# The y sums of the first batch with both halves of the channels side by side, in an order made anew

## The chip, the core and the metric

One core of a Trainium2 chip runs the kernel. TensorE (PE) multiplies matrices, and its weight loads are listed as PEld; VectorE (DVE), ScalarE (ACT) and GpSimd (POOL) do the rest of the arithmetic, and SyncE (SP) issues the transfers. The metric is the time on the device in microseconds (us), as a median of runs.

## The reference, cut to what matters

The program is an attention, a mixing of tokens, and a gated block, for 2 batches of 768 tokens and 512 channels. All arithmetic is float32. The change lies in the middle part:

```
x = attention(q, k, v)                # windows of 16 keys and 24 block summaries; 8 heads of 64
theta = x @ w_theta
zr, zi = x * cos(theta), x * sin(theta)
y = einsum('ts,bsd->btd', w_tok_r, zr) + einsum('ts,bsd->btd', w_tok_i, zi)
u = x + y
x = u + max(u @ w_ch, 0)              # then the gated block: w_in, gelu, layer norm, w_sg, w_out
```

## The kernel before

Every float32 product is made of three matmuls: each operand is split into a high and a low part (`mm3`, lines 650 to 652). `x` is kept transposed in `xT`, channels on the partitions.

**The attention** has 16 units: 8 pairs of heads (`at_pair`), each in 2 halves of the tokens (`at_unit`). A unit is a chain through the engines: scores `S` on PE, row maxima `m` and differences `P` on DVE, the exponential on ACT, transposes `PT` on PE, their copies `Pt`, the values `O` on PE, the normalisation (`ri`, then `x`) on DVE, a transpose `X` on PE and its copy into `xT`. The scores of all units share one pair of PSUM banks (kind "S" of the pools; the six other banks are of kind "B"), so that a unit's scores wait for the differences of the unit before. `k`, `q`, `vT` and `v` of each unit come by DMA, as do all weights.

**The mixing.** For each block of 128 tokens `n` (6 for each batch) `theta` makes `th` on PE; ACT and DVE take off whole turns (`kk`, `rr`). For each half of the channels, `h`, `rotated` makes sine and cosine (tile `f`), multiplies them by `x`, and splits the products into high and low (tile `z`). `mixed` adds a block's `z` into the sums. The output of a 128-channel group `d` has 768 tokens: the first 512 lie in a bank `y`, the other 256 (the rest) in half of a bank `ys`. A step of the sums is six matmuls, three of 512 columns into `y` and three of 256 into `ys`, and there are two steps (weights `w_r` and `w_i`) for each of the two groups of a half:

```
for i in range(NT):                 # NT = 6 blocks of tokens
    for j in range(2):              # d = 2 * h + j
        for k_, key_ in enumerate(("r", "i")):
```

Before, `mixed` runs once for each batch and half: all six blocks for the first half of the channels, then all six for the second. It holds three banks at a time. When the last step is done, DVE adds the sums to `xT` (`uv`).

**The order** of all instructions is made when the program is built. `Order.play` is a planner: each operation has estimated costs, a due time (`key`, drawn from the table `PLAN` or from what depends on it, less a lead from `LEAD`), and a shift of its own (`SHIFT`). The planner plays the engines forward and takes, on each, the most urgent operation that could start soon. Where PE would idle between 6 and 36 us of its reckoning, it puts in dummy matmuls (`fill_B`, from `filler`). `gates` hold back the making of `z` so that it isn't more than a few blocks ahead of the sums.

After the mixing come `ch` (the product with `w_ch`), `iv` and `iu` (the two halves of `w_in`), `Qs` (the product with `w_sg`), and `o` (`w_out`), whose parts are stored as they are done.

Of the kernel before, what the change touches and what calls it, by code (L numbers as in the profile page):

```python
# [22 lines left out]
NT = S // P  # L23
# [25 lines left out]
    Qz=74.168, ks=-40.136, vs=-11.881, vm=11.936, vr=-13.929, e=17.901, Pt=48.07, n=-10.669,  # L49
    xe=4.677, xh=9.148, xl=4.343, kk=-1.1, rr=-29.76, sc=-13.602, zm=-9.187, zh=7.556, zl=38.914,  # L50
    w_tht=8.728, w_rt=13.865, w_it=-1.048, w_rit=-8.999, k=-3.022, q=-3.059, v=1.199, vT=9.157,
    w_rd=22.528, w_id=-5.655, w_rid=3.014, w_thd=-9.579, bsg=-5.815, ch_e=13.7, d=14.634,
    gagf=-1.524, gh=8.649, gl=15.226, gm=-10.408, iu_g=88.574, iv_g=-16.768, m=-33.701,
    o_e=-19.883, rv=-3.588, sq=1.118, st=-55.633, tx=-19.318, tx_h=10.785, u=-3.396, u_h=-9.153,
    uv=-43.926, vh=6.864, vl=9.675, vo=-7.023, vp=0.039, w_chd=6.133, w_chh=-0.456, w_chl=3.459,
    w_chr=-13.975, w_cht=58.117, w_ih=-5.761, w_il=-46.919, w_inud=10.646, w_inuh=12.592,
    w_inul=-13.707, w_inur=8.343, w_inut=57.665, w_invd=15.806, w_invh=-50.158, w_invl=-21.398,
    w_invt=-8.855, w_ir=22.177, w_outd=-25.619, w_outh=15.605, w_outl=-21.45, w_outr=6.525,
    w_outt=12.079, w_rh=5.347, w_rih=6.258, w_ril=-15.3, w_rir=-13.172, w_rr=-12.082,
    w_sgd=9.125, w_sgh=5.251, w_sgl=6.738, w_sgsd=-2.394, w_sgsh=-4.109, w_sgsl=-4.009,  # L60
    w_thh=-3.486, ab=-11.929, o_ae=-17.964, o_be=5.444, w_invr=-3.314, w_rl=6.746, w_thl=8.414,
    w_thr=-2.869, Qaa=-36.615, Qab=18.479, Qac=-4.476, Qad=32.953, Qba=-7.182, Qbb=-4.881,
    Qbc=-45.244, Qbd=0.242, Qd=-14.617, Qe=15.488, Qg=4.768, Qh=-3.207, Qk=-11.256, Ql=5.491,
    Qm=10.937, Qu=-4.014, Qv=11.136, Qw=28.942, Qxh=5.023, Qxl=-5.36, gc=0.703, gt=2.997,
    gw=24.853, Qn=-29.771, Qx=-8.957, Qyh=1.69, Qyl=-22.283)
# [4 lines left out]
    warm0=(3.965, 0), masks0=(-3.862, 0), sets=(3.556, 0), masks2=(1.455, 0),  # L70
    cst=(15.845, 2.915), fill=(-9.642, 0), w_th0d=(-3.673, 15.198), w_th0t=(2.45, 0),
    w_th0r=(-.408, 0), w_th0h=(-1.22, 0), w_th0l=(.268, 0), w_th1d=(-1.914, -18.157),
    w_th1t=(1.029, 0), w_th1r=(-1.741, 0), w_th1h=(1.156, 0), w_th1l=(-.234, 0),
    w_th2d=(1.529, 5.971), w_th2t=(1.909, 0), w_th2r=(-1.914, 0), w_th2h=(-1.157, 0),
    w_th2l=(-.108, 0), w_th3d=(4.03, -1.082), w_th3t=(-2.527, 0), w_th3r=(-.575, 0),
    w_th3h=(-1.077, 0), w_th3l=(1.202, 0), w_r0d=(-.168, -2.081), w_r0t=(.588, 0),
    w_r0r=(-1.087, 0), w_r0h=(1.116, 0), w_r0l=(-1.655, 0), w_i0d=(-1.155, 15.003),
    w_i0t=(4.861, 0), w_i0r=(1.493, 0), w_i0h=(.108, 0), w_i0l=(-1.832, 0),
    w_ri0d=(3.082, -21.492), w_ri0t=(-7.525, 0), w_ri0r=(-.588, 0), w_ri0h=(-4.096, 0),
    w_ri0l=(-4.15, 0), w_r1d=(2.146, 10.79), w_r1t=(2.919, 0), w_r1r=(-1.704, 0),  # L80
    w_r1h=(-1.983, 0), w_r1l=(-1.058, 0), w_i1d=(-1.983, 11.44), w_i1t=(.641, 0),
    w_i1r=(4.405, 0), w_i1h=(-1.438, 0), w_i1l=(3.002, 0), w_ri1d=(.07, -2.92),
    w_ri1t=(-5.223, 0), w_ri1r=(.001, 0), w_ri1h=(-.079, 0), w_ri1l=(5.236, 0),
    w_r2d=(-7.111, -10.609), w_r2t=(.053, 0), w_r2r=(4.47, 0), w_r2h=(-5.26, 0),
    w_r2l=(-2.052, 0), w_i2d=(11.782, -14.445), w_i2t=(4.916, 0), w_i2r=(-.222, 0),
    w_i2h=(1.104, 0), w_i2l=(-1.867, 0), w_ri2d=(-1.883, 3.84), w_ri2t=(-.804, 0),
    w_ri2r=(-.544, 0), w_ri2h=(-5.231, 0), w_ri2l=(-2.723, 0), w_r3d=(-1.364, -8.117),
    w_r3t=(-3.117, 0), w_r3r=(4.499, 0), w_r3h=(-7.344, 0), w_r3l=(-5.466, 0),
    w_i3d=(7.147, 1.379), w_i3t=(-2.77, 0), w_i3r=(-5.827, 0), w_i3h=(-8.506, 0),
    w_i3l=(4.281, 0), w_ri3d=(-12.998, -22.098), w_ri3t=(1.16, 0), w_ri3r=(-2.26, 0),  # L90
    w_ri3h=(.737, 0), w_ri3l=(.496, 0), w_r4d=(6.596, -7.956), w_r4t=(-4.96, 0), w_r4r=(.092, 0),
    w_r4h=(.009, 0), w_r4l=(-10.529, 0), w_i4d=(-11.202, -6.738), w_i4t=(-1.817, 0),
    w_i4r=(-8.488, 0), w_i4h=(-1.595, 0), w_i4l=(.021, 0), w_ri4d=(6.591, -2.316),
    w_ri4t=(-.414, 0), w_ri4r=(1.569, 0), w_ri4h=(-3.272, 0), w_ri4l=(4.015, 0),
    w_r5d=(12.123, 3.875), w_r5t=(-2.799, 0), w_r5r=(.332, 0), w_r5h=(-.403, 0),
    w_r5l=(-12.426, 0), w_i5d=(8.685, 2.603), w_i5t=(2.874, 0), w_i5r=(-10.224, 0),
    w_i5h=(7.798, 0), w_i5l=(-2.331, 0), w_ri5d=(1.821, -1.805), w_ri5t=(-2.508, 0),
    w_ri5r=(6.718, 0), w_ri5h=(-.537, 0), w_ri5l=(3.889, 0), w_ch0d=(19.331, -7.138),
    w_ch0t=(6.055, 0), w_ch0r=(.748, 0), w_ch0h=(-3.195, 0), w_ch0l=(2.036, 0),
    w_inv0d=(9.499, -8.007), w_inv0t=(5.274, 0), w_inv0r=(.996, 0), w_inv0h=(4.98, 0),  # L100
    w_inv0l=(-2.049, 0), w_inu0d=(-13.818, -1.564), w_inu0t=(-1.458, 0), w_inu0r=(-2.338, 0),
    w_inu0h=(-.759, 0), w_inu0l=(-2.165, 0), w_out0d=(15.204, -.19), w_out0t=(-1.162, 0),
    w_out0r=(2.291, 0), w_out0h=(.433, 0), w_out0l=(-1.945, 0), w_ch1d=(16.728, -2.047),
    w_ch1t=(7.412, 0), w_ch1r=(2.329, 0), w_ch1h=(-5.061, 0), w_ch1l=(-2.158, 0),
    w_inv1d=(4.343, 25.037), w_inv1t=(4.333, 0), w_inv1r=(-4.484, 0), w_inv1h=(-6.68, 0),
# [441 lines left out]
def kernel(  # L547
# [106 lines left out]
    def sl(c, n=P):  # L654
        return slice(c * n, (c + 1) * n)
# [944 lines left out]
```

## Time and profile before

| what | us |
|---|---|
| median of 3 runs | 382.21 |
| lowest and highest of them | 379.33, 382.38 |
| the profiled execution, whole | 380.85 |
| its span, first to last instruction | 379.1 |
| PE busy in the span | 369.4 |
| DVE, ACT, POOL busy | 261.6, 204.1, 120.1 |

The profile is of one execution; 1.75 us of its time lie outside its span. A matmul's end is modelled, so that rows of consecutive matmuls overlap by some tenths of a microsecond, and the pitch is read from start to start. "Issue" in a column of waits means that no event in the profile explains the wait.

### The profile page before, as it was taken

The page shows a single profiled execution, that of the slowest core. Times are in us where ns is not written, and L with a number is a line of the kernel's source. Part 1 is how long each engine was busy: PE and PEld are TensorE (multiplying, and loading weights), DVE is VectorE, ACT ScalarE, POOL GpSimd, SP SyncE. Part 2 cuts the span into 40 slices and gives each one's busy share as a digit, 9 for nine tenths or more (in the row PEclk, how much of TensorE's full clock was granted, in tenths as well). Part 3 has the DMA queues.
Part 4 walks back from the last instruction along what each step waited for, and adds up shares of the span by engine and source line. Part 5 has one row for each costly group of instructions (what it writes and reads, how often), then busy time and mean ns, then how long its engine had stood idle before and what let it go on. Part 6 is the DMA issues. An engine that isn't in the chain of part 4 may idle for free.

```text
span 379.1 us, 7679 instructions
## 1 busy us (share of the span) xinstructions
PE 369.4 (97%) x2991; PEld 321.9 (85%) x2991; DVE 261.6 (69%) x453; ACT 204.1 (54%) x349; POOL 120.1 (32%) x145
## 2 busy tenths in 40 slices
PE   8898999999999999999999999999999999999996
PEld 4786888888888888888888788888888999999996
DVE  4997999999975964436674968684134487689621
ACT  2586699967874862234743862458234876332100
POOL 6663488553310200002620163335000046521000
PEclk9998999999999999999999999999999999999999
DMA  7999897992005041002556921646021443511222
GB/s 267 334 338 305 297 315 191 316 345 70 0 9 215 2 145 62 2 0 80 182 171 240 355 99 64 228 158 218 0 83 43 125 144 106 158 52 58 91 103 84
DMA packets 27332, 57.38 MB, mean 151 GB/s; under 512 B 3424, under 2 KB 16800, under 8 KB 27296
## 3 DMA queue, kind: packets, MB, share of 16 engines
q1 hardware_dynamic: 27296, 56.90, 44.9%
q8 instruction: 23, 0.38, 0.4%
q14 instruction: 13, 0.11, 0.1%
HBM read 45.18 MB, written 11.40 MB: 149 GB/s over the span
## 4 chain that ended last, share of the span: by engine, by line
PE 82%; DMA 5%; DVE 5%; ACT 3%; issue 2%; POOL 1%; SPq 1%; POOLq 0%; DVEq 0%; ACTq 0%
PE y L650 6%; PE y L651 6%; PE y L652 6%; PE Qs L650 3%; PE Qs L651 3%; PE Qs L652 3%; PE ch L650 3%; PE ys L651 3%; PE ch L651 3%; PE ys L652 3%; PE iu L652 3%; PE iu L651 3%; PE ch L652 3%; PE iu L650 3%; PE iv L652 3%; PE iv L651 3%
## 5 line engine op out<-in xcount | busy, mean ns | idle before, releaser
L645 DVE TENSOR_TENSOR z<-f,z 128x512 fp32r<-128x512 f32 x21 | 14.9, 709 | 20.8 <-ACT z L637 20.6
L650 PE MATMUL Qs<-Qx,Qh 128*128 128x384 f32 x84 | 28.2, 336 | 0.2 <-DVE U L1458 0.2
L652 PE MATMUL Qs<-Qx,Ql 128*128 128x384 f32 x84 | 28.1, 334 | 0.0
L651 PE MATMUL Qs<-Qx,Qh 128*128 128x384 f32 x84 | 28.1, 334 | 0.0
L652 PE MATMUL ys<-w_ri,z 128*128 128x256 f32 x96 | 27.1, 282 | 0.0
L651 PE MATMUL ys<-w_ri,z 128*128 128x256 f32 x96 | 27.1, 282 | 0.0
L650 PE MATMUL ys<-w_ri,z 128*128 128x256 f32 x96 | 26.7, 278 | 0.0
L637 ACT ACTIVATE z<-f 128x512 fp32r<-128x512 f32 x19 | 11.9, 627 | 23.7 <-PE ys L652 18.1
L650 PEld LDWEIGHTS ys<-w_ri,z 128*128 128x128 f32 x96 | 18.0, 188 | 4.4
L637 ACT ACTIVATE Qx<-Qx 128x768 fp32r<-128x768 f32 x20 | 16.6, 843 | 9.3 <-DMA Qx<-dQx 6.4
L651 PEld LDWEIGHTS ys<-w_ri,z 128*128 128x128 f32 x96 | 18.0, 188 | 3.8
L650 PE MATMUL th<-w_th,xh 128*128 128x512 f32 x48 | 20.6, 428 | 0.2 <-DVE xT L642 0.2
L1061 DVE TENSOR_TENSOR f<-f,x 128x512 f32<-128x512 f32 x21 | 16.0, 763 | 5.4 <-ACT f L1055 5.1
L652 PE MATMUL th<-w_th,xh 128*128 128x512 f32 x48 | 19.3, 402 | 0.3 <-DVE xh L645 0.3
L650 PE MATMUL y<-w_i,z 128*128 128x512 f32 x48 | 19.3, 402 | 0.0
L651 PE MATMUL th<-w_th,xh 128*128 128x512 f32 x48 | 19.3, 401 | 0.0
L650 PE MATMUL y<-w_r,z 128*128 128x512 f32 x48 | 19.2, 399 | 0.0
L651 PE MATMUL y<-w_r,z 128*128 128x512 f32 x48 | 19.0, 397 | 0.0
L651 PE MATMUL y<-w_i,z 128*128 128x512 f32 x48 | 19.0, 395 | 0.0
L645 DVE TENSOR_TENSOR Ql<-vx,Qh 128x768 fp32r<-128x768 f32 x10 | 9.4, 960 | 13.7 <-PE iu L652 9.4
L650 PE MATMUL ch<-u,w_ch 128*128 128x512 f32 x48 | 18.8, 392 | 0.0
L650 PE MATMUL iu<-tx,w_inu 128*128 128x512 f32 x48 | 18.7, 390 | 0.0
(357 smaller groups left out, 1174.2 us busy)
## 6 DMA issues: line engine op xcount, KB each, us to landing
Qx<-dQx SPq DMA_DIRECT2D x21, 384.0 KB, 3.7
v<-in_vW_dram SPq DMA_DIRECT2D x16, 193.5 KB, 5.1
k<-in_kT_dram SPq DMA_DIRECT2D x8, 384.0 KB, 6.5
q<-in_qT_dram SPq DMA_DIRECT2D x16, 192.0 KB, 5.0
vT<-in_vT_dram SPq DMA_DIRECT2D x8, 384.0 KB, 5.2
w_r<-in_w_rT_dram SPq DMA_DIRECT2D x6, 511.8 KB, 5.0
w_i<-in_w_iT_dram SPq DMA_DIRECT2D x6, 511.8 KB, 5.6
Qw<-in_w_sgT_dram SPq DMA_DIRECT2D x12, 192.0 KB, 2.5
```

The source lines that it names most:

```text
L637: ACT.activation(dst, src, AF.Copy, scale=scale)
L645: EN[e].tensor_tensor(out=lo, in0=src, in1=hi.bitcast(F32), op=ALU.subtract)
L650: PE.matmul(ps, ah, bh, start=first, stop=False, skip_group_check=True)
L651: PE.matmul(ps, ah, bl, start=False, stop=False, skip_group_check=True)
L652: PE.matmul(ps, al, bh, start=False, stop=last, skip_group_check=True)
L1061: EN[e].tensor_tensor(out=z3(), in0=z3(), in1=x.unsqueeze(1).to_broadcast([P, 2, 256]), op=ALU.mult)
```

## The change

For batch 0 `mixed` is called once with both halves of the channels: block by block, it makes the eight steps of the four groups. It holds four "B" banks for `y0` to `y3`, and the four rests lie in the pair of banks of kind "S", which is the scores' until the attention is over. Batch 1 is summed as before. `turn`, from which the gates are drawn, follows the new order of batch 0. DVE's additions to `xT` now wait for the last step of their own half.

The planner gets a reckoning of PE's instruction supply: `fetch` counts instructions by operation (`CODE`), supposes that blocks of 256 are asked for 200 instructions before they are needed and come 3.3 us later, and adds what PE would wait. Two estimated costs are new. `PLAN`, `LEAD` and nearly all entries of `SHIFT` have other numbers, which gives every engine another order. The matmuls are the same but for the dummy ones: 16 `fill_B` in place of 9.

```diff
-    q_from=121.281, q_step=28.693, q_back=223.53, at0=-10.9, at0_pair=7.346, at0_half=2.395,
+    q_from=88.069, q_step=27.528, q_back=242.693, at0=-26.358, at0_pair=4.729, at0_half=3.964,
...
+    FETCH = 3.3
+    BLOCK, ASK, HAVE = 256, 246, 446
+    CODE = {"M": 10, "L": 48, "S": 104, "O": 48, "PT": 6, "X": 6, "th": 6, "y": 12, "vp": 2, "Qp": 18,
+            "fill": 10}
...
+    def fetch(self, n, d, s):
+
+        late, at, end = 0.0, self.at, self.at + n
+        while True:
+            ask = self.ASK + self.BLOCK * len(self.come)
+            have = self.HAVE + self.BLOCK * self.had
+            if ask <= have:
+                if ask >= end:
+                    break
+                t = s + late + max(0, ask - at) * d / n
+                self.come.append(max(t, self.come[-1] if self.come else 0.0) + self.FETCH)
+            else:
+                if have >= end:
+                    break
+                t = s + late + max(0, have - at) * d / n
+                late += max(0.0, self.come[self.had] - t)
+                self.had += 1
+        self.at = end
+        return late
...
+            if e == "PE":
+                if n > 0 and self.FILL_FROM < s < self.FILL_TO:
+                    self.fetch(2 * n, n * self.FILL, free_at["PE"])
+                code = "".join(c for c in o.name if not c.isdigit()).strip("_")
+                f += self.fetch(self.CODE.get(code, 24), o.eng[e], s)
...
-    def mixed(b, h, key, step):
+    def mixed(b, hs, key, step):
+        both = len(hs) > 1
         pre = last[0]
+        def rest(h, j):
+            return (f"ys{b}", 512 * h + 256 * j) if both else (f"ys{b}_{h}", 256 * j)
         for i in range(NT):
             n = b * NT + i
+            for q, (h, j, k_) in enumerate((h, j, k_) for h in hs for j in range(2) for k_ in range(2)):
...
+                    if j == 0 and h == hs[0]:
+                        new.append((ys, "S" if both else "B"))
...
+                    op(f"uv{b}_{d}_{half}", {"DVE": dve(w)}, ev,
+                       after=[f"y{b}_{NT - 1}_{2 * h + 1}_1"],
+                       use=[f"y{b}_{d}" if half == 0 else ys])
...
-    turn = [(b, h, i) for b in range(B) for h in range(2) for i in range(NT)]
+    turn = ([(0, h, i) for i in range(NT) for h in range(2)]
+            + [(1, h, i) for h in range(2) for i in range(NT)])
...
-    mixed(0, 0, PLAN["y00"], PLAN["y00_step"])
-    mixed(0, 1, PLAN["y01"], PLAN["y01_step"])
-    mixed(1, 0, PLAN["y10"], PLAN["y10_step"])
-    mixed(1, 1, PLAN["y11"], PLAN["y11_step"])
+    mixed(0, (0, 1), PLAN["y00"], PLAN["y00_step"])
+    mixed(1, (0,), PLAN["y10"], PLAN["y10_step"])
+    mixed(1, (1,), PLAN["y11"], PLAN["y11_step"])
```

Three places show the order on the engines; a row is a line of the code, an instruction, what it writes and reads, and its shape (x12: twelve in a row).

**PE, from the seventh unit's scores to the eighth's.** Before:

```order
L890 MATMUL S_0_680<-k_320,q_0_451 64x96 x12
L890 MATMUL S_0_680<-ks_478,q_0_451 64x24 x12
L942 MATMUL PT_1_0_719<-ident,P_1_669 120x128 x3
L942 MATMUL PT_1_1_726<-ident,P_1_669 120x128 x3
L980 MATMUL X_0_732<-ident,x_0_429 128x128 x3
L957 MATMUL O_1_741<-v_1_525,Pt_1_0_730 64x65 x6
L957 MATMUL O_1_741<-v_1_525,Pt_1_1_738 64x65 x6
L881 LDWEIGHTS identb
```

and now:

```order
L923 MATMUL S_0_675<-k_444,q_0_289 64x96 x12
L923 MATMUL S_0_675<-ks_640,q_0_289 64x24 x12
L990 MATMUL O_0_710<-v_0_534,Pt_0_0_638 64x65 x6
L990 MATMUL O_0_710<-v_0_534,Pt_0_1_632 64x65 x6
L975 MATMUL PT_1_0_728<-ident,P_1_662 120x128 x3
L975 MATMUL PT_1_1_736<-ident,P_1_662 120x128 x3
L1013 MATMUL X_1_744<-ident,x_1_531 128x128 x3
L990 MATMUL O_1_755<-v_1_496,Pt_1_0_740 64x65 x6
L990 MATMUL O_1_755<-v_1_496,Pt_1_1_751 64x65 x6
L914 LDWEIGHTS identb
```

One more unit's values stand between the two scores now; every listed matmul of scores or values is executed as two.

**DVE, the end of the attention**, up to the last normalisation (`w_ri1r` is a weight on its way to high and low parts, `xh` the split of batch 1's `x`). Before, rows 126 to 137 of its list:

```order
L766 SCALAR_TENSOR_TENSOR w_ri1r<-w_ri_1446,zero_185 128x512
L766 SCALAR_TENSOR_TENSOR w_r3r<-w_r_1077,zero_183 128x512
L642 COPY xT<-X_0_1716 128x384
L967 TENSOR_SCALAR ri_1_1747<-O_1_1666 128x6
L968 RECIPROCAL ri_1_1747<-ri_1_1747 128x6
L971 TENSOR_TENSOR x_1_1422<-O_1_1666,ri_1_1747 128x3x128
L645 TENSOR_TENSOR xh_1751<-xT,xh_1751 128x512
L645 TENSOR_TENSOR xh_1753<-xT,xh_1753 128x512
L645 TENSOR_TENSOR w_ri_1730<-w_ri1r,w_ri_1730 128x512
L967 TENSOR_SCALAR ri_1_1775<-O_1_1734 128x6
L968 RECIPROCAL ri_1_1775<-ri_1_1775 128x6
L971 TENSOR_TENSOR x_1_1422<-O_1_1734,ri_1_1775 128x3x128
```

and now, rows 114 to 124:

```order
L675 COPY Pt_1_0_1668<-PT_1_0_1647 120x384
L799 SCALAR_TENSOR_TENSOR w_ri0r<-w_ri_1490,zero_185 128x512
L1000 TENSOR_SCALAR ri_1_1692<-O_1_1655 128x6
L1001 RECIPROCAL ri_1_1692<-ri_1_1692 128x6
L1004 TENSOR_TENSOR x_1_1446<-O_1_1655,ri_1_1692 128x3x128
L1000 TENSOR_SCALAR ri_0_1716<-O_0_1674 128x6
L1001 RECIPROCAL ri_0_1716<-ri_0_1716 128x6
L1004 TENSOR_TENSOR x_0_1381<-O_0_1674,ri_0_1716 128x3x128
L1000 TENSOR_SCALAR ri_1_1733<-O_1_1698 128x6
L1001 RECIPROCAL ri_1_1733<-ri_1_1733 128x6
L1004 TENSOR_TENSOR x_1_1446<-O_1_1698,ri_1_1733 128x3x128
```

The last normalisation has moved from row 137 to row 124: weights, a copy and the splits of `x` that stood ahead of it now come behind.

**PE, in the sums of batch 0**, as one step ends and the next begins (`z_0` is of the first half of the channels, `z_1` of the second). Before:

```order
L650 MATMUL y_1_1756<-w_i_1888,z_0_1542 128x512
L651 MATMUL y_1_1756<-w_i_1888,z_0_1542 128x512
L652 MATMUL y_1_1756<-w_i_1888,z_0_1542 128x512
L650 MATMUL ys_0_1530<-w_ri_1799,z_0_1542 128x256
L651 MATMUL ys_0_1530<-w_ri_1799,z_0_1542 128x256
L652 MATMUL ys_0_1530<-w_ri_1799,z_0_1542 128x256
L650 MATMUL y_0_1526<-w_r_1732,z_0_1882 128x512
L651 MATMUL y_0_1526<-w_r_1732,z_0_1882 128x512
L652 MATMUL y_0_1526<-w_r_1732,z_0_1882 128x512
L650 MATMUL ys_0_1530<-w_ri_1898,z_0_1882 128x256
L651 MATMUL ys_0_1530<-w_ri_1898,z_0_1882 128x256
L652 MATMUL ys_0_1530<-w_ri_1898,z_0_1882 128x256
```

and now:

```order
L683 MATMUL y_1_1782<-w_i_1760,z_0_1327 128x512
L684 MATMUL y_1_1782<-w_i_1760,z_0_1327 128x512
L685 MATMUL y_1_1782<-w_i_1760,z_0_1327 128x512
L683 MATMUL ys_1753<-w_ri_1828,z_0_1327 128x256
L684 MATMUL ys_1753<-w_ri_1828,z_0_1327 128x256
L685 MATMUL ys_1753<-w_ri_1828,z_0_1327 128x256
L683 MATMUL y_2_1888<-w_r_1807,z_1_1909 128x512
L684 MATMUL y_2_1888<-w_r_1807,z_1_1909 128x512
L685 MATMUL y_2_1888<-w_r_1807,z_1_1909 128x512
L683 MATMUL ys_1753<-w_ri_1828,z_1_1909 128x256
L684 MATMUL ys_1753<-w_ri_1828,z_1_1909 128x256
L685 MATMUL ys_1753<-w_ri_1828,z_1_1909 128x256
```

Where the next block of the same half followed, the other half of the same block follows now, and all rests go to the one tile `ys`.

## Rows read from the trace of the kernel before

**Rows 1.** The page, parts 1 and 3: busy us, share, instructions; packets, MB.
```profile
PE 369.4 (97%) x2991; PEld 321.9 (85%) x2991; DVE 261.6 (69%) x453; ACT 204.1 (54%) x349; POOL 120.1 (32%) x145
...
q8 instruction: 23, 0.38, 0.4%
```

**Rows 2.** Windows of PE: stretch, length, busy (instructions), clock, DMA share, GB/s.
```profile
0.00:6.20 6.20, 4.95 (x59) 1.00 0.67 220
6.20:30.70 24.50, 22.09 (x542) 1.00 1.04 336
30.70:41.58 10.88, 9.16 (x117) 0.84 0.86 282
41.58:71.90 30.32, 29.91 (x546) 1.00 0.88 277
71.90:100.00 28.10, 27.66 (x295) 1.00 0.53 188
100.00:375.90 275.90, 275.64 (x1450) 1.00 0.33 111
```

**Rows 3.** Waits of PE: line, waited for, total us, times, longest.
```profile
PE S L881 <- DVE P L929: 1.3, 4, 0.4
```

**Rows 4.** Timeline of PE to 90 us: start, us, instructions, [idle before].
```profile
6.19 2.00 PE L710 MATMUL fill_B<-maskb,identb 128*128 128x480 bf16 x9
...
30.25 0.50 PE L890 MATMUL S<-k,q 64*64 64x96 f32 x14
32.46 0.41 PE L890 MATMUL S<-k,q 64*64 64x96 f32 x9 [1.72 <-issue]
...
43.44 0.40 PE L650 MATMUL th<-w_th,xh 128*128 128x512 f32 x1
43.67 0.39 PE L651 MATMUL th<-w_th,xh 128*128 128x512 f32 x1
...
71.91 0.47 PE L650 MATMUL y<-w_r,z 128*128 128x512 f32 x1
...
75.66 3.02 PE L957 MATMUL O<-v,Pt 120*64 120x65 f32 x96
...
89.64 0.82 PE L980 MATMUL X<-ident,x 128*128 128x128 f32 x6
```

**Rows 5.** Windows of all engines: PE, PEld, DVE, ACT, POOL busy, clock, DMA.
```profile
0.00:30.75 30.75, 27.08 (x596) 20.82 (x597) 24.29 (x43) 18.31 (x32) 19.61 (x44) 1.00 0.96 312
34.00:36.00 2.00, 2.00 (x7) 1.68 (x6) 1.93 (x6) 1.40 (x4) 0.00 (x0) 0.50 0.95 310
```

**Rows 6.** DVE's groups by line and shape: busy us, mean ns, idle before.
```profile
L1061 DVE TENSOR_TENSOR f<-f,x 128x512 f32<-128x512 f32 x21 | 16.0, 763 | 5.4 <-ACT f L1055 5.1
L645 DVE TENSOR_TENSOR z<-f,z 128x512 fp32r<-128x512 f32 x21 | 14.9, 709 | 20.8 <-ACT z L637 20.6
L1031 DVE TENSOR_TENSOR rr<-th,kk 128x512 f32<-128x512 f32 x12 | 8.2, 683 | 0.7 <-ACT kk L1026 0.5
...
L642 DVE COPY xT<-X 128x384 f32<-128x384 f32 x6 | 3.2, 546 | 0.0
...
L837 DVE TENSOR_REDUCE vs<-vT 128x24 f32<-128x768 f32 x3 | 2.8, 941 | 0.0
...
L766 DVE SCALAR_TENSOR_TENSOR w_r5r<-w_r,zero 128x512 int32<-128x512 int32 x1 | 0.7, 686 | 0.0
```

**Rows 7.** Timeline of DVE: the last normalisation of the attention.
```profile
85.99 0.56 DVE L971 TENSOR_TENSOR x<-O,ri 128x384 f32<-128x384 f32 x1
```

**Rows 8.** Timeline of PE, 100 to 102 us: two steps of the y sums.
```profile
100.37 0.40 PE L650 MATMUL y<-w_i,z 128*128 128x512 f32 x1
...
101.42 0.40 PE L650 MATMUL y<-w_r,z 128*128 128x512 f32 x1
```

**Rows 9.** Timeline of SP's queue: the first issue of the weights' rests.
```profile
51.41 0.82 SPq L748 DMA_DIRECT2D w_ri<-in_w_rT_dram  x1
```

**Rows 10.** Timeline of PE, the last matmul.
```profile
375.58 0.27 PE L652 MATMUL o_3a<-gx,w_out 128*128 128x192 f32 x1
```

More of the change, by code (lines that the diff above doesn't have):

```diff
@@ L50 @@
[L50 to L59, printed above, removed]
-    w_sgd=9.125, w_sgh=5.251, w_sgl=6.738, w_sgsd=-2.394, w_sgsh=-4.109, w_sgsl=-4.009,
-    w_thh=-3.486, ab=-11.929, o_ae=-17.964, o_be=5.444, w_invr=-3.314, w_rl=6.746, w_thl=8.414,
@@ L1070, in rotated, with mm @@
            after=[f"zh{m}"], use=[f"f{m}", f"z{m}"], port=PORT)
-    def mixed(b, h, key, step):
+    def mixed(b, hs, key, step):
+        both = len(hs) > 1
         pre = last[0]
+        def rest(h, j):
+            return (f"ys{b}", 512 * h + 256 * j) if both else (f"ys{b}_{h}", 256 * j)
         for i in range(NT):
             n = b * NT + i
+            for q, (h, j, k_) in enumerate((h, j, k_) for h in hs for j in range(2) for k_ in range(2)):
+                d, key_ = 2 * h + j, "ri"[k_]
+                ys, c0 = rest(h, j)
+                def mm(e, n=n, i=i, j=j, d=d, h=h, k_=k_, key_=key_, ys=ys, c0=c0):
+                    z = T(f"z{n}_{h}")
+                    a = [z[:, o + 256 * k_ + 128 * j:o + 256 * k_ + 128 * j + 128]
+                         for o in (0, 512)]
+                    mm3(T(f"y{b}_{d}")[:], a, units[key_, i], i == 0 and k_ == 0,
+                        i == NT - 1 and k_ == 1)
+                    mm3(T(ys)[:, c0:c0 + 256], a, cut(units["ri", i], sl(k_, 256)),
+                        i == 0 and k_ == 0 and j == 0, i == NT - 1 and k_ == 1 and j == 1)
+                new, use = [], [f"z{n}_{h}", wu(key_, i), wu("ri", i)]
+                if i == 0 and k_ == 0:
+                    new.append((f"y{b}_{d}", "B"))
+                    if j == 0 and h == hs[0]:
+                        new.append((ys, "S" if both else "B"))
+                    else:
+                        use.append(ys)
+                else:
+                    use += [f"y{b}_{d}", ys]
+                nm = f"y{b}_{i}_{d}_{k_}"
+                op(nm, {"PE": 1.055}, mm, after=[f"zl{n}_{h}", wn(key_, i), wn("ri", i)] + pre,
+                   new=new, use=use, key=key + (i + q / (4 * len(hs))) * step,
+                   spare=PLAN["y_spare"] if new else 0)
+                pre = [nm]
+        last[0] = pre
+        for h in hs:
@@ L1102, in mixed @@
-        last[0] = pre
-        for j in range(2):
-            d = 2 * h + j
-            for half, (o, w) in enumerate(HALVES):
-                def ev(e, d=d, j=j, half=half, o=o, w=w):
-                    ps = T(f"y{b}_{d}")[:] if half == 0 else T(f"ys{b}_{h}")[:, sl(j, 256)]
-                    dst = xT[:, d, b * S + o:b * S + o + w]
-                    DVE.tensor_tensor(out=dst, in0=ps, in1=dst, op=ALU.add)
-                op(f"uv{b}_{d}_{half}", {"DVE": dve(w)}, ev, after=pre,
-                   use=[f"y{b}_{d}" if half == 0 else f"ys{b}_{h}"])
+                ys, c0 = rest(h, j)
@@ new lines, in mixed, with ev @@
+                for half, (o, w) in enumerate(HALVES):
+                    def ev(e, d=d, half=half, o=o, w=w, ys=ys, c0=c0):
+                        ps = T(f"y{b}_{d}")[:] if half == 0 else T(ys)[:, c0:c0 + 256]
+                        dst = xT[:, d, b * S + o:b * S + o + w]
+                        DVE.tensor_tensor(out=dst, in0=ps, in1=dst, op=ALU.add)
+                    op(f"uv{b}_{d}_{half}", {"DVE": dve(w)}, ev,
+                       after=[f"y{b}_{NT - 1}_{2 * h + 1}_1"],
+                       use=[f"y{b}_{d}" if half == 0 else ys])
@@ L1220, in norm @@
                                       op1=ALU.mult)
-            op(f"vo{b}_{i}", {"ACT": act(512), "DVE": 0.54}, norm, after=[f"rv{b}"], use=[vx],
+            op(f"vo{b}_{i}", {"ACT": 0.8, "DVE": 0.54}, norm, after=[f"rv{b}"], use=[vx],
                port=("DVE",))
@@ L1377, in gated @@
             if (half, f // 2) != (0, 0):
-                op("Qn" + tag, {"DVE": dve(384)},
+                op("Qn" + tag, {"DVE": 0.61},
                    lambda e: DVE.scalar_tensor_tensor(
```

648 lines of the change are left out of this document (320 added, 328 removed).

## The prediction

> **What bounds the kernel now.** I read the page first: PE is busy for 369.4 of a span of 379.1 us, in 2,991 matmuls with as many weight loads, and no other engine comes near it [rows 1]. The windows of PE then show where it isn't busy. From 100 us to the last matmul at 375.58 it loses 0.26 us in 276 [rows 2, 10]. An order can win nothing back there; whatever is gained or lost is decided in the first 100 us, and is then carried to the end.
>
> There PE idles for 1.25 us in the first 6.2 (most of it start), 2.41 up to 30.7, 1.72 up to 41.58, 0.41 up to 71.9, 0.44 up to 100 [rows 2]. With the 0.26 that is 6.49. Two losses hide inside busy time. Nine dummy matmuls take 2.00 us [rows 4], 0.222 each. And in the stretch from 30.7 to 41.58 the granted clock is 0.84 on average, and 0.50 (1.2 GHz) from 34 to 36 [rows 2, 5]: 10.88 x 0.16 = 1.74 us lost. All that could ever be had by order alone is 6.49 - 1.25 + 2.00 + 1.74 = 8.98 us, which would end at 371.9. The work itself (the pitch of the matmuls, their number) isn't touched.
>
> The timeline of PE shows that two of these losses are one event. At 30.75, in the middle of the eighth unit's scores (14 matmuls done of 24), PE stops for 1.72 us, and no event explains it [rows 4]. It is the longest hole of the span. Behind it the clock is at half. Together they cost 1.72 + 1.74 = 3.46 us. By then 596 matmuls and 597 weight loads had run [rows 5], 1,193 instructions. A queue of its own moves PE's code: 23 packets, 0.38 MB [rows 1], for 5,982 instructions, so some 260 in each. A stop without a releaser, while the DMA engines are at a share of 1.04 [rows 2], looks like code that came late.
>
> **The change part by part.** *The sums themselves* cost nothing and bring nothing. There are 96 steps before and after, each of three matmuls of 512 columns and three of 256, at 1.05 us from one step to the next [rows 8]. That both halves alternate doesn't alter the pitch, since each matmul loads its own weights in either case.
>
> *Banks.* Batch 0 now holds four of the six single banks, where it held three, and the pair. Two are left for theta. A block of theta is 12 matmuls at 0.23 [rows 4], 2.7 us, and its bank is free again after `kk` and `rr` (`rr` 0.683 [rows 6], `kk` about the same): the next block in the other bank hides that. The pair is taken only after the last scores (row 336 of PE's list; the sums begin at row 364), so nobody waits for it: 0. If scores stood behind the first step, they would wait for the whole batch, some 50 steps.
>
> *Supply of z.* A block now asks DVE for `rr` and two of each of `f` and `z`, 0.683 + 2 x (0.763 + 0.709) = 3.6 us [rows 6], and gives PE 8 x 1.05 + 2.7 = 11.1 us of work. Before, one half gave 4.2 + 2.7. There is more cover than before: 0, and no gain, since PE didn't wait there.
>
> *The end of the attention* is the place where the order matters. DVE's last normalisation is at 85.99 to 86.55 [rows 7], and PE took the last `X` at 89.64 [rows 4]. Ahead of it DVE now has less to do: one `rr` (0.683), three copies into `xT` (0.546), two sums of `vT` (0.941), five operations on weights (0.686), by counting both lists, 0.68 + 1.64 + 1.88 + 3.43 = 7.6 us [rows 6]. PE has 24 matmuls of theta and two steps of the sums less ahead of its last `X`, 24 x 0.23 + 2 x 1.05 = 7.6 us. So both arrive earlier by the same, and what was put off comes later, where PE has no holes. If PE also gains the 3.46, it reaches `X` at 78.6 and DVE's result is there at 78.9, before its copy of the gain. The new wait is between 0 and 1.6 us (two links of that chain, 0.56 to 0.8 each, late); I take 0.5.
>
> *Transfers.* The first rests of weights (`w_ri`) stand 3.4 MB later in SP's queue, by the sizes in its list. They were issued at 51.41 [rows 9]; at 277 GB/s [rows 2] that is 12 us later, 63.5. The first step of the sums, at 71.91 before [rows 4], comes at about 79. Landing and splitting have 15 us: 0.
>
> *Dummies.* Seven more, 7 x 0.222 = 1.55 us. Where PE would wait anyway they cost 0, where it wouldn't they cost all. I take half, 0.78.
>
> *The stop at 30.75.* The order around it is new, with one more unit's values between the seventh and the eighth scores. Between 0 and 3.46 us are won. I take all of it, because the stop is single: everywhere else the same kind of stretch runs through, as at 75.66, where 96 matmuls of values with as many loads go by in 3.02 us [rows 4]. The place needs bad luck of timing, and the timing changes.
>
> The Trainium skill ("Runtime: NRT & Kernel Launch", Instruction fetch mechanics) says that code comes in blocks of 256 instructions, and that crossing a block's edge is mostly hidden; it also gives PE room for 2,048 instructions. The first sentence agrees with some 260 in a packet [rows 1]. The second speaks against this change: with 2,048 in store, a stop at the 1,193rd would not be late code, and no count of instructions would move it. By that the sum would lack the 3.46.
>
> Sum against the profiled execution: 380.85 - 3.46 + 0.78 + 0.50 = 378.7. That execution lies 1.36 below the median of 382.21, and the three runs spread over 3.05. Half of that difference is likely to stay in a median of new runs, so I say **379.3**, 0.8% below the median.
>
> **The rivals.** *The stop stays* (the change doesn't do what its planner's new reckoning is for). For it: counted in the new list, the 1,193rd instruction again falls into the eighth unit's scores, a stretch just as dense, while the DMA engines are as full as before. Against: the stop came once, and its neighbours a packet earlier and later passed. Time: 380.85 + 0.78 + 0.50 = 382.1, no change. The Trainium skill's store of 2,048 instructions (same page and section) would make this the outcome; a hole at the 1,193rd that nothing explains [rows 4] bears it out only in part, since it leaves the hole without a cause.
>
> *Two new stops: slower.* In the new list the 2,217th and the 2,473rd instruction (four and five blocks of 256 behind the 1,193rd) fall into the scores of three neighbouring units, rows 279 to 313, with only transposes and values between, where blocks of theta stood before. The planner supposes a block to be asked for 200 instructions ahead; at the pace of 75.66 (192 in 3.02 us) these last 3.1 us. If a block of code takes longer, PE stops at both, at 3.46 each with its clock: 382.1 + 6.9 = 389.0 with the old stop left, 385.6 without. For it: the DMA share was still 0.88 there [rows 2]. Against: the run of values at 75.66, just as dense, had no hole. It decides at about 3.1 us of delivery.
>
> *More is won.* PE waits 1.3 us for `P` in four places [rows 3], and 2.41 up to 30.7. If half of these and of the dummies go too, 378.7 - 2.5 = 376.2 or less.
>
> **How the numbers follow.** Forecast (377.5 to 381.2) 0.42; the stop stays, or half of it does (381.2 to 384) 0.26; new stops 0.14; more won 0.18. A measurement of this kernel can tell about 1% from no change, 3.8 us: faster is below 378.4, slower above 386.0. Faster: 0.18 and a little less than half of the forecast's, 0.37. Slower: most of the new stops and a bit of other new waits, 0.15. The rest is 0.48. The range leaves out a tenth on either side: from 375 (more won, down to about two thirds of the 8.98) to 386.
>
> **What would show it.** Right: no hole without a releaser between 20 and 45 us, granted clock at 1.00 there, the last normalisation at 76 to 80 us, the first `y` at 78 to 81, and from there no idle PE. Wrong: a hole in the scores at the same count; holes in the windows from 50 to 70; PE waiting for `Pt`, `x` or `xh` between 70 and 82; a half-rate clock anywhere behind 10 us; or a pitch of the y steps other than 1.05, which would mean that the sums' new order touches PE's speed after all.

## The result, and the profile after

The changed kernel is slower by 1.0%: 384.46 us against 380.15 in the median (20 executions of each), a ratio of 1.0102, interval 1.0081 to 1.0123. The ratio leaves out two executions of the changed kernel that lie over 1.5% above its fastest; the medians of all differ by 1.1%. The 382.21 of the three first runs was high for the kernel before. The profiled execution of the changed kernel took 383.04 us, with a span of 381.2.

The page of the changed kernel, its first and third part:

```profile
PE 369.8 (97%) x2998; PEld 320.7 (84%) x2998; DVE 269.9 (71%) x460; ACT 203.2 (53%) x352; POOL 111.3 (29%) x143
...
q8 instruction: 23, 0.38, 0.4%
```

PE is busy as long as before [rows 1], though up to its last matmul no half clock is in this execution: the seven more dummies add about what the clock took before. The windows of PE, cut as in [rows 2] and further on (stretch, length, busy and matmuls, clock, DMA share, GB/s):

```profile
30.70:41.58 10.88, 9.47 (x169) 1.00 0.89 301
71.90:100.00 28.10, 27.33 (x224) 1.00 0.65 225
100.00:140.00 40.00, 40.00 (x223) 1.00 0.19 67
300.00:340.00 40.00, 38.02 (x218) 1.00 0.41 139
```

From 30.7 to 41.58 us PE still loses 1.41. In the stretch from 300 us on, which lost next to nothing before, it loses 1.98. The waits of PE in the whole span, cut to four rows:

```profile
PE Qs L683 <- DVE R L1500: 2.0, 1, 2.0
PE S L923 <- issue: 1.8, 2, 1.4
...
PE S L914 <- DVE P L962: 1.1, 3, 0.4
PE O L990 <- DMA v<-ones: 0.8, 1, 0.8
...
```

The third row answers to [rows 3], the second to the stop in [rows 4] and a short one of 0.36 at 20 us; the first and the last are new. The timeline of PE at the places named:

```profile
31.13 0.49 PE L923 MATMUL S<-k,q 64*64 64x96 f32 x10
33.02 0.47 PE L923 MATMUL S<-k,q 64*64 64x96 f32 x11 [1.41 <-issue]
...
77.10 2.11 PE L990 MATMUL O<-v,Pt 120*64 120x65 f32 x65 [0.77 <-DMA v<-ones]
...
100.73 0.40 PE L683 MATMUL y<-w_r,z 128*128 128x512 f32 x1
101.78 0.40 PE L683 MATMUL y<-w_i,z 128*128 128x512 f32 x1
...
332.86 0.41 PE L683 MATMUL Qs<-Qx,Qh 128*128 128x384 f32 x1 [1.98 <-DVE R L1500]
```

The stop without a releaser is where it was, in the eighth unit's scores, behind ten matmuls of 24 in place of 14 [rows 4]. Counted by the windows, again exactly 596 matmuls and 597 weight loads have run [rows 5]:

```profile
0.00:31.55 31.55, 28.00 (x596) 1.00 0.95 308
0.00:31.55 31.55, 20.85 (x597) 1.00 0.95 308
```

The first of the two is the window of PE, the second that of PEld. A step of the y sums still takes 1.05 us [rows 8]. What is new lies at 331 us. The timeline of DVE there:

```profile
327.17 0.61 DVE L1421 SCALAR_TENSOR_TENSOR R<-R,g_sb,bsg 128x384 f32<-128x384 f32 x1
327.82 0.63 DVE L1430 TENSOR_TENSOR R<-R,ut 128x128 f32<-128x128 f32 x2
328.36 0.61 DVE L1421 SCALAR_TENSOR_TENSOR R<-R,g_sb,bsg 128x384 f32<-128x384 f32 x1
329.10 0.98 DVE L678 TENSOR_TENSOR g<-R,g 128x384 fp32r<-128x384 f32 x1
330.01 2.24 DVE L1430 TENSOR_TENSOR R<-R,ut 128x128 f32<-128x128 f32 x2
332.17 1.01 DVE L1500 TENSOR_TENSOR R<-Qs,R 128x384 f32<-128x384 f32 x2
```

The last row is `Qe1_1_5` and `Qe1_0_5`, the additions that empty the banks of two gate sums (`Qs`) of batch 1. PE wants the first of these banks again one sum later, at 330.9, and gets it at 332.86. On DVE they stand behind `Qk0_1_2` (329.10) and `Qm0_1_3` (330.01), work for batch 0 that PE needs later. `Qm0_1_3` is two products, which took 2.24 us together; the row at 327.82 has the same shapes and 0.63. GpSimd makes `Ql` beside them:

```profile
329.76 2.00 POOL L678 TENSOR_TENSOR Ql<-vx,Qh 128x768 fp32r<-128x768 f32 x1
```

So the wait has two parts: with 0.63 the additions would have come 1.61 earlier, and some 0.4 of the 1.98 would be left. This is an estimate from these rows; no run moved `Ql`. In the kernel before, two sums into another pair of banks lay between the last use of this bank and the next: 18 matmuls at a pitch of 0.173, 3.1 us of cover in place of 1.6, and no wait stood here.

### The profile page after: what moved, and what is told of

The parts are those of the page before. It is cut to its first block, busy times and chain, and to the rows that moved or that the text cites. A ratio compares the mean times of both kernels' runs of the same rounds, so it can differ in the third digit from the quotient of the medians.

```text
span 381.2 us, 7712 instructions
## 1 busy us (share of the span) xinstructions
PE 369.8 (97%) x2998; PEld 320.7 (84%) x2998; DVE 269.9 (71%) x460; ACT 203.2 (53%) x352; POOL 111.3 (29%) x143
## 4 chain that ended last, share of the span: by engine, by line
PE 74%; DVE 11%; DMA 7%; ACT 5%; issue 2%; SPq 1%; DVEq 0%; ACTq 0%
PE y L683 4%; PE y L684 4%; PE y L685 4%; PE iu L685 3%; PE iu L684 3%; PE iv L685 3%; PE iv L683 3%; PE iu L683 3%; PE iv L684 3%; PE Qs L683 3%; PE Qs L685 3%; PE Qs L684 3%; PE o L683 3%; PE o L685 3%; PE o L684 3%; PE ch L683 2%
## 5 line engine op out<-in xcount | busy, mean ns | idle before, releaser
L685 PE MATMUL ys<-w_ri,z 128*128 128x256 f32 x96 | 27.1, 282 | 0.0
L684 PE MATMUL ys<-w_ri,z 128*128 128x256 f32 x96 | 27.1, 282 | 0.0
L1233 DVE BATCH_NORM_STATS2 st<-vx 128x6 f32<-128x512 f32 x12 | 8.3, 688 | 21.1 <-ACT vx L1223 21.1
L678 DVE TENSOR_TENSOR z<-f,z 128x512 fp32r<-128x512 f32 x19 | 13.5, 710 | 13.5 <-ACT z L670 12.8
L672 POOL TENSOR_SCALAR Qh<-vx 128x768 fp32r<-128x768 f32 x7 | 6.3, 898 | 52.3 <-PE iu L685 28.2
L683 PE MATMUL th<-w_th,xh 128*128 128x512 f32 x48 | 19.9, 414 | 0.0
L956 DVE TENSOR_REDUCE m<-S 128x6 f32<-128x720 f32 x16 | 14.4, 903 | 7.0 <-PE S L923 7.0
L1094 DVE TENSOR_TENSOR f<-f,x 128x512 f32<-128x512 f32 x18 | 14.9, 829 | 6.1 <-ACT f L1088 6.0
L684 PE MATMUL th<-w_th,xh 128*128 128x512 f32 x48 | 18.8, 392 | 0.0
```

Source lines behind the costliest of these rows:

```text
L672: POOL.tensor_scalar(out=dst, in0=src, scalar1=scale, scalar2=0.0, op0=ALU.mult, op1=ALU.add)
L678: EN[e].tensor_tensor(out=lo, in0=src, in1=hi.bitcast(F32), op=ALU.subtract)
L683: PE.matmul(ps, ah, bh, start=first, stop=False, skip_group_check=True)
L684: PE.matmul(ps, ah, bl, start=False, stop=False, skip_group_check=True)
L685: PE.matmul(ps, al, bh, start=False, stop=last, skip_group_check=True)
L956: DVE.tensor_reduce(out=T(f"m{u}")[:, :6].rearrange("p (h t) -> p h t", h=2), in_=s4(), axis=AX.X, op=ALU.max)
```

## The experiments

Where an experiment moves operations, the list that the planner gives is kept, and only the named ones are taken out and put back elsewhere. The first such edit, written out; the later ones name the operations and their new place:

```diff
-    for o in order.play():
-        o.fn(o.on)
+    seq = order.play()
+    part = [o for o in seq if o.name in ('Qe1_1_5', 'Qe1_0_5')]
+    seq = [o for o in seq if o not in part]
+    at = [o.name for o in seq].index('Qk0_1_2')
+    seq[at:at] = part
+    for o in seq:
+        o.fn(o.on)
```

**a_qs: the two additions go forward.** 

> The changed kernel with one move: on VectorE the second additions of the gate's sums Qe1_1_5 and Qe1_0_5 stand ahead of the gate product Qk0_1_2 and the product Qm0_1_3 of the other batch, which in the changed kernel they stand behind. Theory A (the slower time is the new place of instructions on VectorE near 330 us): TensorE's wait for the addition R L1500 near 331 us, 1.98 us, falls to under 0.3 us, the last matmul ends 1.6 to 2.0 us earlier, and the profiled span is 379.2 to 379.6 us at a clock of 1.00. The median falls by 1.7 to 3.5 us, more than the wait where a stop that long also lowers the clock in part of the executions. Rival (it is given back): VectorE is busy enough there that the two moved products are then the late ones; the wait turns up at another sum behind 332 us, and the time falls by less than 0.7 us. Rival B (the two halves side by side cost TensorE more from 100 us on): the time stays where it is whatever VectorE does.

Measured: 381.96 us (12 executions), ratio to the kernel before 1.0055 (1.0029 to 1.0080), span of the profile 378.7. The timeline of DVE:

```profile
327.58 0.61 DVE L1421 SCALAR_TENSOR_TENSOR R<-R,g_sb,bsg 128x384 f32<-128x384 f32 x1
328.58 1.02 DVE L1500 TENSOR_TENSOR R<-Qs,R 128x384 f32<-128x384 f32 x2 [0.38 <-PE Qs L685]
329.52 1.72 DVE L678 TENSOR_TENSOR g<-R,g 128x384 fp32r<-128x384 f32 x1
```

The additions now run at 328.58, as soon as PE has the sums, and PE no longer waits. The median fell by 2.5, as theory A said. Rival B, that the time stays whatever DVE does, fails. Some 2.2 us to the kernel before are left. Of the waits, the second here is new, and stood hidden behind the long one:

```profile
PE O L990 <- DMA v<-ones: 1.2, 1, 1.2
...
PE o L683 <- DVE o_1s L1538: 0.6, 1, 0.6
```

**a_both: on SyncE, also `vm6`, `vr6_1`, `vr6_0` ahead of `w_ri1d`.** 

> The run before this one with one more move: on SyncE the two spreads of the value ones of the seventh pair (vr6_1, vr6_0) go ahead of the two loads of w_ri1, with the small copy vm6 that they need. Theory A: the wait of the values O for DMA v<-ones at 77.1 us, 0.77 us, is gone, since the spreads are issued near 68.4 us and no longer at 70.5 us, and the time is 0.5 to 0.8 us under that run's. Rival (given back): TensorE has slack from 77 to 100 us in which it would have waited in any case, for the operands z of the sums or for w_ri1, which now comes 1.7 us later; then the same within 0.3 us.

Measured: 382.01, no better than a_qs. The wait for `v<-ones` is gone from the profile, the time is not, within what 12 executions can tell. A possible reason was seen when the same kernel ran again (a_both_2, below).

**b_split: is the stop a matter of count or of place?**

```diff
-            PE.matmul(ps[:, :5 * WK], identb[:], maskb[:].rearrange("p k c -> p (k c)"), start=True, stop=True)
+            for m in range(5):
+                PE.matmul(ps[:, m * WK:(m + 1) * WK], identb[:], maskb[:, m, :], start=True, stop=True)
```

> The kernel before, with each dummy matmul of 480 columns made in five of 96 (the same columns, 72 instructions more, all ahead of 8 us). Theory C (the stop of 1.72 us at 30.75 us belongs to the count of TensorE's instructions, which are brought in late at that point): it stays behind the 596th recorded matmul, and so moves 72 instructions back in the work, from the 8th unit's scores into the values O of the 7th unit, at 29.3 to 29.8 us; its length stays at 1.4 to 1.9 us. Rival (it belongs to the place: the 8th unit's scores wait for something that the records don't show, such as an operand): it stays in the 8th unit's scores at 30.5 to 31 us, now behind some 632 matmuls. The time stays within 1 us of the kernel before by both.

Measured: 380.31, ratio 1.0007 (0.9982 to 1.0033). The stop left the eighth unit's scores, but didn't go to the seventh unit's values either. The timeline of PE:

```profile
23.65 0.24 PE L891 MATMUL S<-ks,q 64*64 64x24 f32 x3
25.42 0.54 PE L891 MATMUL S<-ks,q 64*64 64x24 f32 x21 [1.54 <-issue]
```

The window of PE up to it:

```profile
0.00:24.60 24.60, 20.97 (x471) 1.00 0.93 298
```

It now stands behind 471 matmuls and 472 weight loads, 943 instructions: 250 ahead of 1,193, so one block earlier. Both expectations missed. What holds is the grid: a stop can stand at the edge of a block of some 256 instructions. Which edge comes late isn't settled by this run. Place alone is ruled out.

**s_struct: the new code with the old tables (`PLAN`, `LEAD`, `SHIFT` of the kernel before).** 

> The code of the changed kernel (both halves of the channels side by side in the first batch, rests in a pair of banks, instruction blocks in the planner's sums) with the tables of numbers of the kernel before. Theory A (the new form of the sums is free, the order is what costs): TensorE's busy time from 100 us on is that of the kernel before within 0.5 us, no wait of 2 us stands near 330 us since the order there comes from the old numbers, and the time is decided by whatever waits these numbers leave in the first 150 us, for which they weren't made: 378 to 384 us. Rival B (the form costs): the sums of the first batch take longer each, or wait for z or for a bank, by 2 us or more in all, with the rest of the program as in the kernel before: 382 us or more.

Measured: 399.41. Its waits are 5.3 us at one `y` for `z`, 3.1 at one `Qs`, 5.6 in seven scores. By the letter rival B holds (a wait for `z` of over 2 us, a time of over 382), and theory A's 378 to 384 is missed. But the run tells little of the form's cost, since these numbers were made for another order, as A also said; it does show what waits do to the clock: the granted clock is 0.94 in the window from 140 to 200 us, and 0.96 from 300 to 340. Without that, its `ys` matmuls take what they always took (medians of 278 to 283 ns).

**a_again: the changed kernel once more.** 

> The changed kernel once more, for a second profile of it. Theory A (the stop at instruction 1,193 belongs to the kernel, and its length to the execution): a stop stands behind the same 596 or so recorded matmuls in the 8th unit's scores, with another length between 0.2 and 2 us, and the wait of 1.98 us near 331 us stands again within 0.1 us, since it comes from the order of VectorE alone. Rival: both lengths differ, and the waits of the changed kernel are chance.

Measured: 384.81, 1.77 above the first profile. The two waits agree with that one to 0.02 us (1.41 in the scores, 1.97 at 331 us). The difference lies in the windows of PE behind the second:

```profile
330.00:333.00 3.00, 1.11 (x7) 1.00 0.39 131
333.00:334.00 1.00, 0.92 (x5) 0.91 0.02 8
334.00:335.00 1.00, 1.00 (x5) 0.50 0.08 16
335.00:336.00 1.00, 1.00 (x5) 0.50 0.00 0
336.00:337.00 1.00, 1.00 (x4) 0.50 0.00 0
337.00:338.00 1.00, 1.00 (x6) 0.88 0.00 0
```

The clock fell to 0.50, 1.2 GHz, from about 333.8 to 337.2, which costs 0.09 + 3 x 0.50 + 0.12 = 1.71 us. In the first profile the same wait left the clock at 1.00. So the wait of 2 us cost 2 us in both, and 1.7 more in one of them. The wait at 331 us is the order's, as theory A has it; the stop's length, which A let vary, was the same here (1.41), and differs in other runs.

**a_three2: also `o01_1e` ahead of `Qm1_1_1` on VectorE.** 

> The run a_both with one more move: on VectorE the addition o01_1e, which empties the bank of the out-projection's second tile, goes one instruction forward, ahead of the product Qm1_1_1, so 0.47 us earlier. In the run a_both TensorE waited 0.88 us for it at 342.6 us; in the changed kernel this stood hidden behind the wait of 2 us at 331 us. Theory A (each wait behind 60 us is paid in full and comes from the order alone): the wait is 0.3 to 0.5 us, the median falls by some 0.4 us from 382.0 us. Rival (the rest of the distance to the kernel before, some 2 us, lies in the first 35 us, in the seven more dummies and the stop): the wait shrinks, and the median stays at 381.5 to 382.5 us.

Measured: 379.87, ratio 0.9990 (0.9958 to 1.0022): level with the kernel before. The fall of 2.1 from a_both was five times what was expected, and side by side it didn't repeat (a_both_2). The wait for `o_1s` is 0.6, not 0.3 to 0.5. Moved further, ahead of `Qn1_1_1`, the addition makes a program whose engines wait for one another without end (a_three, and a_three_nine without the later dummies); these two have no time.

**a_nine2: that, without the later seven dummies.** The edit skips the three operations `fill8.95`, `fill16.39` and `fill24.89`. 

> The run a_three2 without the seven later dummies (two at 9.6 us, three at 17.2 us, two at 26.0 us); the first nine stay. Theory A (the dummies cost what they last, 7 by 0.22 us, where no wait stands behind them): the scores of the 8th unit begin 0.8 to 1.5 us earlier and the median falls by as much, to some 380.5 us. Rival C (the stop at instruction 1,193 ends at a time that the fetch sets, not TensorE): 14 instructions fewer stand ahead of it, it moves 14 instructions on in the work, within the 8th unit's scores, and ends at 32 to 33 us as before, so that what the dummies took is added to the stop, which is then 2.2 to 3.0 us long, and the median falls by less than 0.4 us.

Measured: 380.78, ratio 0.9999 (0.9964 to 1.0033), beside a_three2's 379.87: no gain that can be told, with some 1.3 us to either side in each interval. Rival C named the place to the matmul, though not the length. The timeline of PE:

```profile
31.16 0.57 PE L923 MATMUL S<-k,q 64*64 64x96 f32 x17
33.36 0.31 PE L923 MATMUL S<-k,q 64*64 64x96 f32 x4 [1.63 <-issue]
...
68.54 0.53 PE L923 MATMUL S<-ks,q 64*64 64x24 f32 x18 [1.46 <-issue]
```

PE waited 1.8 us for `P` and 1.2 for `q` ahead of it, where a_three2 has 1.3 and 0.6. So in these two profiles 1.1 of the 1.55 us that the dummies took went into those. The second stop, at 68.54, is at a new place, behind 1,228 matmuls and as many loads, 2,456 instructions.

**a_quiet: a_three2 with five loads issued later, by ScalarE.** `q5_0`, `k5`, `w_r0d`, `k7`, `q6_0` (`LATE` below) go ahead of `w_th3r`, and their loads use `nc.scalar`; one of three such lines:

```diff
-            nc.sync.dma_start(T(f"k{p}")[:, :S], kT[b, r])
+            (nc.scalar if f'k{p}' in LATE else nc.sync).dma_start(T(f"k{p}")[:, :S], kT[b, r])
```

> The run a_three2 with five loads (q5_0, k5, w_r0d, k7, q6_0; 1.66 MB) that SyncE issues from 28.1 to 32.5 us issued later, by ScalarE near 35 us, so that fewer transfers are under way while the instructions of the 8th unit's scores are fetched. Theory D (the fetch is late since the transfers hold the DMA engines, whose mean share is 0.96 from 25 to 32 us): the stop behind 596 recorded matmuls shrinks from 1.4 to 1.7 us to under 0.6 us, and the time falls by 0.8 to 1.5 us, or by less where the later loads or ScalarE's issues make units 4 to 7 wait. Rival E (the fetch takes a fixed time, and TensorE runs through the instructions ahead of it faster than that): the stop keeps its 1.4 to 1.7 us.

Measured: 383.98, with a stop of 1.69 us, and a new wait of 2.6 us of `th` for a copy into `xT` on ACT, which spends 34.70 to 38.25 on the issues. By the letter rival E holds, but the test was weak. The windows of PE (last figures: DMA share, GB/s):

```profile
30.00:32.00 2.00, 1.30 (x38) 1.00 0.97 362
32.00:34.00 2.00, 1.02 (x40) 1.00 0.38 128
```

Transfers issued earlier kept the DMA engines full to 32 us, and the stop ended at 32.98. Whether full engines make the code late stays open.

**a_two: the second and third move without the first.** 

> The changed kernel with the second and the third move (the spreads vr6 on SyncE, o01_1e on VectorE) but without the first: Qe1_1_5 and Qe1_0_5 stay behind Qk0_1_2 and Qm0_1_3. Theory A: the wait of 2.0 us near 331 us stays, the wait for DMA v<-ones at 77 us is gone, and the median is 2.0 us and a share of the clock's loss (up to 1.7 us in part of the executions) above that of the run with all three moves, some 382.5 to 383.5 us. Rival (what the run with all three moves won over the run with two of them, 2.1 us in the medians where 0.4 us was expected, came from its last move or from chance in the early part of the program, and the first move is worth little beside it): the median is under 381.5 us.

Measured: 384.28 (6 executions), ratio 1.0102 (1.0050 to 1.0155), above the 382.5 to 383.5 of theory A, with the wait back at 331. The timeline of PE:

```profile
333.87 0.41 PE L683 MATMUL Qs<-Qx,Qh 128*128 128x384 f32 x1 [1.98 <-DVE R L1500]
```

Next to a_three2_2, on the same chip, it is 3.6 us slower. The two additions alone carry most of the loss.

**a_both_2 and a_three2_2, repeats.** 

> The run a_both again, beside the run with all three moves on the same chip. Theory A (a move of 0.47 us is worth 0.5 us at most): the two medians lie within 1.0 us of each other, this one above. Rival (the third move is worth 2 us): this one lies 1.5 us or more above.

> The run a_three2 again, with all three moves. Theory A (the order alone makes the difference between the changed kernel and the kernel before): within 1.0 us of the kernel before, 379.5 to 381.3 us. Rival (the form of the sums or the dummies cost 1 us or more): 381.3 us or more.

Measured: 380.95 and 380.66, ratios 1.0020 (0.9987 to 1.0053) and 1.0037 (1.0008 to 1.0067). The third move is worth about 0.3, as theory A has it, so most of the 2.1 was chance. The 380.66 lies within A's 379.5 to 381.3, but 1.3 above the kernel before beside it, where A said 1.0 at most. The profile of a_both_2 is of its slowest execution, 385.87 us, and shows what can stand where the wait for `v<-ones` was. The timeline of PE:

```profile
74.83 0.85 PE L990 MATMUL O<-v,Pt 120*64 120x65 f32 x21
77.42 0.33 PE L990 MATMUL O<-v,Pt 120*64 120x65 f32 x3 [1.73 <-issue]
```

Two windows behind it:

```profile
79.00:80.00 1.00, 1.00 (x4) 0.50 1.04 371
...
81.00:82.00 1.00, 1.00 (x6) 0.50 0.96 340
```

It is again a stop without a releaser, behind 1,354 matmuls and 1,355 loads: 2,709 instructions, 253 behind 2,456. In the changed kernel this edge passes at 73.0 us without a stop, and the wait for `v<-ones` stands 4 us behind it. An execution that stops for 1.7 us at the edge would find the spreads landed, and gain nothing from issuing them earlier. How often that happens isn't shown.

**a_best: a_three2 with the transposes `PT3_0` ahead of the eighth unit's scores.** 

> The run a_three2 with one move on TensorE: the six transposes PT3_0 of the weights of the 7th unit go ahead of the 8th unit's scores, so that the 7th block of TensorE's instructions is first asked for by later work. Theory C (the stop ends at a time that the fetch sets, 32 to 33.3 us): TensorE waits for the exponentials P at 31 us instead, 0.5 to 1.1 us, does the transposes meanwhile, and the stop in the scores is under 0.7 us; the two together are 0.5 to 1.2 us shorter than the stop of 1.4 to 2.2 us, the clock falls in fewer executions, and the median is 0.5 to 1.5 us under that of the run a_three2, near 379 us and under the kernel before. Rival (the stop follows its count): it keeps its 1.4 to 2.2 us behind some 596 recorded matmuls, on top of the wait for P, and the median is 0.5 to 1 us above that of the run a_three2.

Measured: 380.63, ratio 1.0034 (1.0006 to 1.0062): as a_three2_2 on the same chip, and not the 0.5 to 1.5 us less of theory C. The timeline of PE:

```profile
31.79 0.84 PE L975 MATMUL PT<-ident,P 128*120 128x128 f32 x6 [1.01 <-DVE x L1004]
...
33.20 0.63 PE L923 MATMUL S<-k,q 64*64 64x96 f32 x18 [0.17 <-issue]
...
68.28 0.29 PE L923 MATMUL S<-k,q 64*64 64x96 f32 x1 [1.35 <-issue]
...
76.28 0.33 PE L990 MATMUL O<-v,Pt 120*64 120x65 f32 x3 [1.45 <-issue]
```

The first stop is down to 0.17, with a wait of 1.01 in its place, as theory C said. But in this execution the edges at 2,456 (68.28) and 2,709 (76.28) were late in its stead. The mean clock was below 0.998 in only one of its 12 executions. No version is clearly faster than the kernel before.

## Why the prediction was wrong

*"An order can win nothing back there; whatever is gained or lost is decided in the first 100 us".* This step failed. That PE has no idle time behind 100 us says that an order can't win there; it doesn't say that it can't lose. The change made the order anew on every engine to the end, and the sum had no term for the last 280 us. Three DVE instructions in front of two others cost 1.98, and most of it because two of the three ran slowly beside GpSimd. By executions whose mean clock is 0.998 or more, the changed kernel averages 382.63 (6 executions) and a_qs 380.72 (6): 1.91 for the wait.

*The clock.* The prediction counted 1.74 us of it as a loss of the kernel, won back with the stop. It is a chance, taken anew behind each long wait. The median that the forecast is measured by, 382.21 of three executions, was also 2.06 too high: against 380.15, 379.3 is a gain of 0.2% and not of 0.8%. The mean clock was below 0.998 in 14 of 20 executions of the changed kernel and in 5 of 6 of a_two, which keep the long wait; in 24 of 60 where the additions had moved (a_qs, a_both, a_three2, both repeats); and in 32 of 87 of the kernel before. At or under 0.9915, about two falls, the counts are 8 of 26, 3 of 60 and 5 of 87. So the wait at 331 costs 2.0 plus 1.7 in about a third of the executions, 2.6 us of the 4.3.

*The stop at 30.75.* "I take all of it, because the stop is single" was wrong: of the 3.46 to be won, the stop gave 0.31 (1.41 in place of 1.72, in both profiles of the changed kernel). The clock stayed at 1.00 behind it in both, but in the second it fell behind the wait at 331 instead, so about as much as the 1.74 was lost again there. The rival that the stop stays had it right, by the count it gave. Eleven profiles of the changed kernel and its variants have it in the eighth unit's scores, 0.17 to 2.23 us long. The Trainium skill ("Runtime: NRT & Kernel Launch", Instruction fetch mechanics) has PE's code come in blocks of 256 instructions; the counts of 692 (the short stop at 20 us), 943, 1,193, 2,456 and 2,709 in the traces lie on such a grid to within the records that are missing. Its store of 2,048 instructions, weighed against this step, doesn't keep a stop away at 943; here the measurement decides.

That these stops are late code needn't rest on the count alone. The kept traces hold the time of each packet of q8, the queue that moves PE's code [rows 1]. The timelines of the 14 profiles have 23 rows in which PE waits and no event explains it, and in each PE goes on 1.15 to 1.80 us after such a packet has landed. In the kernel before the packet took from 30.07 to 31.18, and PE went on at 32.46; in the changed kernel from 30.69 to 31.74, and PE went on at 33.02. Both packets started less than 1 us before PE stopped; in a_both, where the stop is 0.31, it was 2.7 us before. Why they started so late, no run shows. One of the 23 rows, 0.42 in a_three2_2, stands off the grid, behind 2,666 instructions.

*Two new stops.* The rival put them at the 2,217th and 2,473rd instruction. One place was right: stops at 2,456 recorded came in three variants, 1.46, 1.35 and 0.25 us, not 3.46, and a further one at 2,709 in two, 1.73 and 1.45. The two profiles of the changed kernel itself have neither; how often they come in its other executions can't be seen, nor in those of the kernel before.

*The wait at the end of the attention, 0.50.* Measured 0.77 and 0.86 at 77 us, within the 0 to 1.6. The cause was another: not DVE's chain but the spreads `vr6` on SyncE, which land late. *Dummies, 0.78*: no gain without them that the runs can tell, and most of their time went into other waits; whether it is 0 or 0.78 stays open. *The sums themselves, banks, supply of `z`, transfers at 0*: right. The step is 1.05 us, `ys` takes 27.1 us in 96 matmuls as before, PE waits nowhere for `z`, and for a bank of the sums 0.2 us in all, and the first `y` comes at 81.0 without a wait for `w_ri`.

Of the 4.3 us, the two additions carry 2.6, or 3.6 by a_two against a_three2_2. With all three moves 0 to 1.3 us remain (ratios 0.9990 and 1.0037), which no run resolves further. That the form of the sums has no part in it rests on the pitch and the waits above; no run separates form from order cleanly, s_struct included.

## What to carry to other kernels

When a planner makes a whole order anew, a stretch without idle time is a stretch that can only lose: look, for each bank, how much work lies between its last use and its next, and what stands ahead of the copy that empties it. A wait that is removed may have hidden a later one; only the medians of repeated runs tell, and a gain of 2 us between two sets of 12 executions can be chance here. A profile of one execution shows a half clock or a late block of code as if it were a property of the kernel; take a second profile before pricing it.

## What the runs showed of the hardware

A wait of PE is followed by a half clock in some executions and not in others, with the same instructions and the same wait: 1.98 us without a fall, 1.97 with one, at 331 us. Leaving s_struct and the first 20 us aside, five of seven waits of 1.9 us or more were followed by a clock of 0.50, and three of thirteen between 1.1 and 1.75.

The same first 60 us of instructions gave stops from 0.31 to 1.96 us (a_both and a_both_2, two executions of one kernel).

The two products `Qm0_1_3` on DVE, which read two tiles of SBUF each, took 2.24 us while GpSimd made `Ql` (329.76 to 331.76), and 0.63 at 327.82 for the same shapes. In a_qs it hit `g<-R` instead: 1.72 at 329.52, beside `Ql` from 328.98 to 330.83, where the same shape takes 0.54 at 333.10 of the changed kernel, with GpSimd idle. The Trainium skill ("GPSIMD Engine Reference", Specifications) has GpSimd share its SBUF interfaces with VectorE, to the cost of DVE instructions with two SBUF inputs; the rows agree.
